# Reordering the first two batches of a fused attention and feed-forward kernel, with w_out read in 4 KB runs

## The chip, the cores and the metric

The kernel runs on one core of a Trainium2 chip. The metric is device microseconds (us) of one execution. Inputs are float32 and arrive in device memory; the output is float32. A ratio in this text is the mean time of one kernel's fast runs over the mean of the other kernel's fast runs of the same rounds, so it is not quite the ratio of the medians quoted beside it.

Engine names: PE is the matrix engine, PEld its weight loads, ACT the scalar engine, DVE the vector engine, POOL the general engine, SP the engine that issues nearly all DMA. PSUM is the memory that PE writes its results to; the other engines copy them out. Profile times count from the start of the profiled span.

## The reference, cut to what matters

```python
# q, k, v: (8 batches, 8 heads, 576 positions, 64)
q_s = softmax(q, over the 64)           # per row
k_s = softmax(k, over the 576)          # per column
kv  = k_s.T @ v                         # 64 x 64 per head
x   = q_s @ kv, heads side by side      # 4608 x 512
h   = x @ w_in                          # w_in 512 x 2048
g   = h * sigmoid(beta * h)
out = g @ w_out                         # w_out 2048 x 512
```

Nearly all the work is the two large products `h` and `out` (called `acc` below). For each of nine groups of 512 rows there are 64 matmuls of 128x512 for `h` and 64 for `acc`.

## The kernel before

Nine groups follow one another: one per batch for its first 512 positions, and one for the tails of all batches. While PE works on one group, ACT, DVE and POOL prepare the next one. The first group has no such cover. It needs its q, k and v, and the weights, which arrive in 512-wide blocks of w_in and w_out while it runs. Each block lands in float32 in one of four staging buffers and is then cast to bf16 into a tile that stays.

```python
w_in_b  = const.tile([P, KT, FF], BF16, name="w_in_b")     # 128 x 4 x 2048, one tile
w_out_d = moe_w_out.rearrange("(j p) f -> p j f", p=P)     # 2 KB runs
...
def w_cast(kind, blk, half, eng):
    if kind == "in":
        dst = w_in_b[:, :, ds(blk * 512 + half * 256, 256)]   # 256 columns of each kt
...
def mm_a(c, j, kts=None, tag=None):                        # h block j
    for kt in kts:
        nc.tensor.matmul(h[:], w_in_b[:, kt, ds(j * P, P)], x_of(c)[:, kt, :], ...)
    # then tanh on ACT, then (tanh + 1) * h on DVE -> g
def mm_b(c, j):                                            # acc += g block j @ w_out block j
...
tail_zero(0)
pool_cast(("out", 1), ("in", 2), ("out", 2))               # all casts of later blocks stand here,
tail_zero(1)                                               # ahead of h blocks 4 to 15
pool_cast(("in", 3), ("out", 3))
for u in range(4, NJ):
    mm_a(0, u) ...  mm_b(0, u - LAG) ...                   # and q, k, v of batch 1 in between
```

For the first two batches k and v of two heads lie on the two halves of the partitions. exp(k) is written into a zeroed 128x128 block diagonal, and nine 128-wide matmuls per head pair give kv.

The softmax here doesn't subtract the row's maximum and nothing guards it: scores larger than these inputs give would overflow.

## Time and profile before

| | before |
|---|---|
| median of 3 runs | 288.93 us (288.79 to 290.37) |
| profiled span | 286.8 us |
| PE busy | 97% |
| granted PE clock | 1.000 |
| first `h` matmul / first `acc` matmul | 15.24 / 20.11 us |
| first `h` matmul of batch 1 | 48.75 us |

First the page of the kernel before: the busy time per engine, then the span in 40 slices. A digit is a busy share in tenths; PEclk is the granted clock, DMA the busy share of the DMA engines.

```profile
span 286.8 us, 4132 instructions
...
PE 277.9 (97%) x1595; PEld 127.7 (45%) x1595; DVE 180.0 (63%) x280; ACT 162.9 (57%) x236; POOL 43.7 (15%) x58
...
PE   7799999999999999999999999999999999999994
...
PEclk9999999999999999999999999999999999999999
DMA  7999999809933963296319911893270033005004
```

PE has no hole after the first two slices. DMA is full over the first seven slices, which is the loading of q, k, v and the weights. Next are the groups of the `h` matmuls and of their weight loads (instructions, busy us, mean ns of one; then the idle time of the engine just ahead of them and what ended it).

```profile
L358 PE MATMUL h<-xT,w_in_b 128*128 128x512 bf16 x576 | 146.1, 379 | 0.5 <-ACT xT L143 0.2
...
L358 PEld LDWEIGHTS <-w_in_b 128*128 128x128 bf16 x576 | 55.3, 98 | 67.7 <-issue 2.7
```

The third view is the PE timeline (start, length, what, count).

```profile
20.11 1.89 PE L386 MATMUL acc<-w_out_b,g 128*128 128x512 bf16 x8
21.83 1.89 PE L358 MATMUL h<-xT,w_in_b 128*128 128x512 bf16 x8
23.56 1.89 PE L386 MATMUL acc<-w_out_b,g 128*128 128x512 bf16 x8
25.29 1.03 PE L358 MATMUL h<-xT,w_in_b 128*128 128x512 bf16 x4
...
39.02 0.61 PE L250 MATMUL tp<-identity,eq 128*128 128x128 bf16 x8 [0.62 <-ACT ek L158]
```

Four matmuls take 0.86 us from start to start. The last line has the one wait of note before batch 1, of 0.62 us.

### The profile page before, as it was taken

Reading aid. Unit: us, or ns where it says so; the run is one execution under the profiler, and the core shown is the slowest. Engines: PE = TensorE matmul, PEld = TensorE weight load, DVE = VectorE, ACT = ScalarE, POOL = GpSimd, SP = SyncE. Lnnn points to the kernel's source line nnn. Section 1 sums busy time; section 2 is a strip of 40 time slices with the busy share of each in tenths; the row PEclk is TensorE's granted clock in tenths of the full one; section 3 lists DMA queues with packets and bytes.
Section 4 is the critical chain, followed back from the end, with each engine's and each line's share of the span. In section 5 each row is a group of like instructions: output and inputs, shape, how many; then the busy total and the mean of one; then the engine's idle time right before and its main releaser. Section 6 shows DMA issues by size and latency. Waiting matters only on the chain.

```text
span 286.8 us, 4132 instructions
## 1 busy us (share of the span) xinstructions
PE 277.9 (97%) x1595; PEld 127.7 (45%) x1595; DVE 180.0 (63%) x280; ACT 162.9 (57%) x236; POOL 43.7 (15%) x58
## 2 busy tenths in 40 slices
PE   7799999999999999999999999999999999999994
PEld 2444445444444444444444444444445444444441
DVE  7954597695477457855694469456954695464432
ACT  4763586683496448734773568356835563553341
POOL 4458833300030020001200030003000000000000
PEclk9999999999999999999999999999999999999999
DMA  7999999809933963296319911893270033005004
GB/s 242 377 385 387 371 388 321 280 2 264 280 151 76 313 164 146 46 331 175 127 33 270 269 74 76 194 268 119 115 220 2 1 149 73 0 0 149 0 0 146
DMA packets 56227, 50.08 MB, mean 175 GB/s; under 512 B 26240, under 2 KB 47760, under 8 KB 56208
## 3 DMA queue, kind: packets, MB, share of 16 engines
q1 hardware_dynamic: 56064, 49.56, 55.8%
q8 instruction: 12, 0.20, 0.3%
q10 hardware_dynamic: 144, 0.26, 0.3%
q14 instruction: 7, 0.06, 0.1%
HBM read 36.71 MB, written 9.44 MB: 161 GB/s over the span
## 4 chain that ended last, share of the span: by engine, by line
PE 84%; DMA 11%; SPq 1%; POOL 1%; ACT 1%; issue 0%; DVE 0%; ACTq 0%
PE acc L386 40%; PE h L358 39%; DMA w_in<-in_moe_w_in_dram 6%; DMA k_st<-in_k_dram 5%; PE x L314 2%; PE kv L276 2%; POOL w_in_b L145 1%; PE kv L264 0%; PE tp L250 0%; SPq L85 0%; SPq L106 0%; PE x L318 0%; ACT ek L158 0%; DVE g L370 0%; ACT th L368 0%
## 5 line engine op out<-in xcount | busy, mean ns | idle before, releaser
L368 ACT ACTIVATE th<-h,beta_t 128x512 bf16<-128x512 f32 x144 | 98.5, 687 | 102.6 <-PE h L358 100.7
L370 DVE SCALAR_TENSOR_TENSOR g<-th,h 128x512 bf16<-128x512 bf16 x144 | 97.9, 682 | 92.2 <-ACT th L368 90.7
L358 PE MATMUL h<-xT,w_in_b 128*128 128x512 bf16 x576 | 146.1, 379 | 0.5 <-ACT xT L143 0.2
L386 PE MATMUL acc<-w_out_b,g 128*128 128x512 bf16 x576 | 145.9, 379 | 0.2 <-DVE g L370 0.2
L386 PEld LDWEIGHTS <-g 128*128 128x128 bf16 x576 | 56.0, 98 | 67.9 <-DVE g L370 1.0
L358 PEld LDWEIGHTS <-w_in_b 128*128 128x128 bf16 x576 | 55.3, 98 | 67.7 <-issue 2.7
L145 POOL CAST va<-v_st 128x2048 bf16<-128x2048 f32 (+2 forms) x12 | 17.3, 1460 | 145.0 <-DMA v_st<-in_v_dram 145.0
L225 DVE TENSOR_REDUCE rq<-eq 128x16 f32<-128x1024 bf16 x18 | 21.6, 1198 | 2.3 <-ACT eq L214 2.3
L231 DVE TENSOR_TENSOR eq<-eq,rq 128x1024 bf16<-128x1024 bf16 x18 | 22.6, 1257 | 0.1
L214 ACT ACTIVATE eq<-q_st 128x1024 bf16<-128x1024 f32 x16 | 16.3, 1048 | 2.9 <-DMA q_st<-in_q_dram 2.9
L143 ACT CAST xT<-x 128x512 bf16<-128x512 f32 x20 | 11.6, 585 | 11.1 <-PE x L314 10.3
L169 ACT ACTIVATE ek<-k_st 128x1024 bf16<-128x1024 f32 x12 | 12.6, 1047 | 0.0
L145 DVE COPY o<-acc 128x512 f32<-128x512 f32 x18 | 11.6, 683 | 0.9 <-PE acc L386 0.9
L314 PE MATMUL x<-qsT,kvp 128*128 128x512 bf16 x32 | 11.7, 380 | 0.4 <-DVE kvp L309 0.2
L145 DVE CAST xT<-x 128x512 bf16<-128x512 f32 x16 | 10.9, 684 | 0.5 <-PE x L314 0.5
L143 ACT COPY o<-acc 128x512 f32<-128x512 f32 x18 | 9.7, 591 | 2.6 <-PE acc L386 2.6
L158 ACT ACTIVATE ek<-k_st 64x576 bf16<-64x576 f32 x16 | 10.9, 679 | 0.4
L450 PE MATMUL warm<-kvp 128*128 128x512 bf16 x34 | 9.9, 432 | 1.2 <-DVE kvp L478 1.2
L145 POOL CAST w_out_b<-w_out 128x1024 bf16<-128x1024 f32 x8 | 8.2, 1040 | 6.6 <-DMA w_out<-in_moe_w_out_dram 6.5
L309 DVE TENSOR_TENSOR kvp<-kv,rk 64x256 bf16<-64x256 f32 (+2 forms) x24 | 8.0, 333 | 0.6
L145 POOL CAST w_in_b<-w_in 128x1024 bf16<-128x1024 f32 x7 | 7.2, 1040 | 3.5 <-DMA w_in<-in_moe_w_in_dram 3.4
L450 PEld LDWEIGHTS <-kvp 128*128 128x128 bf16 x34 | 3.4, 108 | 5.3 <-issue 2.1
(38 smaller groups left out, 67.1 us busy)
## 6 DMA issues: line engine op xcount, KB each, us to landing
out_dram<-o SPq DMA_DIRECT2D x14, 512.0 KB, 3.4
q_st<-in_q_dram SPq DMA_DIRECT2D x6, 1024.0 KB, 6.5
k_st<-in_k_dram SPq DMA_DIRECT2D x6, 1024.0 KB, 9.1
v_st<-in_v_dram SPq DMA_DIRECT2D x6, 1024.0 KB, 10.5
w_in<-in_moe_w_in_dram SPq DMA_DIRECT2D x3, 1024.0 KB, 9.7
k_st<-in_k_dram SPq DMA_DIRECT2D x8, 288.0 KB, 7.6
q_st<-in_q_dram SPq DMA_DIRECT2D x4, 512.0 KB, 7.8
w_out<-in_moe_w_out_dram SPq DMA_DIRECT2D x4, 512.0 KB, 9.5
```

What stands on the lines that cost most here:

```text
L143: eng.copy(dst, src)
L145: eng.tensor_copy(dst, src)
L169: nc.scalar.activation(ek[b][:, :, h, :].rearrange("p i h d -> p h i d"), k_st[b][:, h, 0 : R * D].rearrange("p h (i d) -> p h i d", i=R), ...
L214: nc.scalar.activation(eq[b][:, :, s * m : (s + 1) * m, :].rearrange("p i h d -> p h i d"), q_st[b][:, s * m : (s + 1) * m, :].rearrange(" ...
L225: nc.vector.tensor_reduce(rq[b][:, 0, :, h], eq[b][:, :, h, :], axis=AX.X, op=ALU.add)
L231: nc.vector.tensor_tensor(eq[b][:, :, h, :], eq[b][:, :, h, :], rq[b][:, 1, :, h].unsqueeze(3).to_broadcast((P, R, m, D)), ALU.mult,)
L314: nc.tensor.matmul(t[:], kvp[:, c, j, :], qsT[c][:, :, j, :])
L358: nc.tensor.matmul(h[:], w_in_b[:, kt, ds(j * P, P)], x_of(c)[:, kt, :], start=(kt == 0), stop=(kt == KT - 1),)
L368: nc.scalar.activation(th[:], h[:], ACTF.Tanh, scale=beta_t[:, j : j + 1])
L370: nc.vector.scalar_tensor_tensor(out=g[:], in0=th[:], scalar=1.0, in1=h[:], op0=ALU.add, op1=ALU.mult)
L386: nc.tensor.matmul(acc[st][:], g[:, ds(st * P, P)], w_out_b[:, j, :], start=(j == 0), stop=(j == NJ - 1),)
L450: nc.tensor.matmul(t[:, 0:cols], kvp[:, B - 1, 0, :], kvp[:, B - 1, :, :].rearrange("p j r -> p (j r)")[:, 0:cols],)
```

## The change

The intent has five parts. (1) In batches 0 and 1, exp(k) is dense, and kv is computed in two 64x64 quadrants of the array, so no zeroing is needed. (2) Batch 0 starts pair by pair: k and v of one head pair are loaded together, and exp, kv, norm and x follow per pair. (3) w_out is loaded in 4 KB runs, two neighbouring rows to a partition. The columns of `h` have to match, so the weight read of w_in takes every second column. (4) q of batch 1 is loaded ahead of the last weights and its k, v behind them. (5) The end of batch 0 interleaves kv and x of batch 1 with the last `h` and `acc` blocks.

The diff, cut to its core:

```diff
-    w_out_d = moe_w_out.rearrange("(j p) f -> p j f", p=P)
+    w_out_d = moe_w_out.rearrange("(hh p e) f -> p hh e f", p=P, e=2)
+    w_in_u = w_in_b[:].rearrange("p kt (hh q e) -> p kt hh e q", q=P, e=2)
@@ kv_mm, batches 0 and 1
-                    nc.tensor.matmul(t[:, jl, 0:D1], ek[b][:, j, i, :], va[b][:, j, i, :], ...)
+                    for e in range(2):
+                        r = slice(e * D, (e + 1) * D)
+                        nc.tensor.matmul(t[r, jl, 0:D1], ek[b][r, j, ds(i * D, D)], va[b][r, j, i, :],
+                                         ..., tile_position=(e * D, e * D))
@@ mm_a
-                w_in_b[:, kt, ds(j * P, P)],
+                w_in_u[:, kt, j // 2, j % 2, :],
@@ loads
-    load_q(0, parts=2); load_kv(k_st, k, 0, parts=4); load_kv(v_st, v, 0, parts=4); beta
+    q half 0; beta; then per pair j: k pair j, v pair j (q half 1 after pair 0)
-    in 0a, in 0b, out 0a, in 1, out 0b, out 1, in 2, out 2, in 3, q 1, out 3a, k 1, out 3b, v 1
+    in 0a, in 0b, out 0a, out 0b, in 1, out 1, in 2, out 2, q 1, in 3, out 3, k 1 and v 1 by pair
@@ batch 0, second part
-    mm_a 2, 3; mm_b 0, 1; casts of all later blocks; mm_a 4, 5; mm_b 2, 3; ...
+    mm_a 2, 3; casts of all later blocks; mm_b 0, 1, 2, 3; mm_a 4, 5; ...
+    (q transposes, kv, norm and x of batch 1 pair by pair among the last blocks)
```

(The lines under "loads" and "second part" are summaries; the rest is code shortened.)

More of the change, by code (lines that the diff above doesn't have):

```diff
@@ L58 @@
     beta_t = const.tile([P, NJ], F32, name="beta_t")
-    beta_r = const.tile([NJ, P], F32, name="beta_r")
-    ident16 = const.tile([NJ, NJ], F32, name="ident16")
+    beta_r = const.tile([NJ // 2, 2 * P], F32, name="beta_r")
+    ident8 = const.tile([NJ // 2, NJ // 2], F32, name="ident8")
     w_in_b = const.tile([P, KT, FF], BF16, name="w_in_b")
@@ L78, with load_q @@
     g_of, acc_of, att_of = {}, {}, {}
-    def load_q(b, parts=1):
-        t = stage.tile([P, H, R * D], F32, tag="q_st", bufs=2, name=f"q_st{b}")
+    def load_q(b, parts=1, only=None):
+        if b not in q_st:
+            q_st[b] = stage.tile([P, H, R * D], F32, tag="q_st", bufs=2, name=f"q_st{b}")
+        t = q_st[b]
         src = q[b, :, 0:MAIN, :].rearrange("h (p i) d -> p h (i d)", i=R)
         n = H // parts
-        for s in range(parts):
+        for s in range(parts) if only is None else (only,):
             nc.sync.dma_start(t[:, s * n : (s + 1) * n, :], src[:, s * n : (s + 1) * n, :])
-        q_st[b] = t
     def load_qtail():
@@ L97, in load_qtail, with load_kv @@
         q_st[B] = t
-    def load_kv(d, src, b, tag, parts=1):
-        t = stage.tile([P, H * (R + 1) * D], F32, tag=tag, bufs=2, name=f"{tag}{b}")
+    kv_st = {}
+    def load_kv(d, src, b, tag, pairs=None):
+        if (tag, b) not in kv_st:
+            kv_st[tag, b] = stage.tile([P, H * (R + 1) * D], F32, tag=tag, bufs=2, name=f"{tag}{b}")
+        t = kv_st[tag, b]
         if b < NW:
@@ L103, in load_kv @@
             sv = src[b].rearrange("(j e) (p i) d -> (e p) j (i d)", e=2, i=RW)
-            n = HP // parts
-            for s in range(parts):
-                nc.sync.dma_start(d[b][:, s * n : (s + 1) * n, :], sv[:, s * n : (s + 1) * n, :])
+            for j in range(HP) if pairs is None else pairs:
+                nc.sync.dma_start(d[b][:, j, :], sv[:, j, :])
         else:
@@ L126, in w_load @@
         else:
-            src = w_out_d[:, ds(4 * blk, 4), :]
-            c = slice(0, 4) if half is None else slice(half * 2, half * 2 + 2)
-            nc.sync.dma_start(t[:, c, :], src[:, c, :])
+            src = w_out_d[:, ds(2 * blk, 2)]
+            c = slice(0, 2) if half is None else slice(half, half + 1)
+            nc.sync.dma_start(t[:].rearrange("p (hh e) f -> p hh e f", e=2)[:, c], src[:, c])
     def w_cast(kind, blk, half, eng):
@@ L145, in evac, with ek_buf, kz_exp @@
             eng.tensor_copy(dst, src)
-    def ek_buf(b, eng=None):
-        t = work.tile([P, HP * RW * P], BF16, tag="ek", bufs=2, name=f"ek{b}")
+    def ek_buf(b):
+        t = work.tile([P, HP * RW * D], BF16, tag="ek", bufs=2, name=f"ek{b}")
         if b < NW:
-            ek[b] = t[:].rearrange("p (j i m) -> p j i m", j=HP, i=RW)
-            eng.memset(t[:].bitcast(F32), 0.0)
+            ek[b] = t[:].rearrange("p (j r) -> p j r", j=HP)
         else:
             ek[b] = t[:, 0 : R * H * D].rearrange("p (i h d) -> p i h d", i=R, h=H)
-    def kz_exp(b, j, m=1):
-        for e in range(2):
-            r = slice(e * D, (e + 1) * D)
-            nc.scalar.activation(
-                ek[b][r, j : j + m, :, e * D : (e + 1) * D],
-                k_st[b][r, j : j + m, :].rearrange("p j (i d) -> p j i d", i=RW),
-                ACTF.Exp,
-            )
+    def kz_exp(b, j):
+        if j == 0:
+            ek_buf(b)
+        nc.scalar.activation(ek[b][:, j, :], k_st[b][:, j, :], ACTF.Exp)
     def k_exp(b, s, n=2):
@@ L263, in kv_mm @@
                 for i in range(RW):
-                    nc.tensor.matmul(
-                        t[:, jl, 0:D1],
-                        ek[b][:, j, i, :],
-                        va[b][:, j, i, :],
-                        start=(i == 0),
-                        stop=(i == RW - 1),
-                    )
+                    for e in range(2):
+                        r = slice(e * D, (e + 1) * D)
+                        nc.tensor.matmul(
+                            t[r, jl, 0:D1],
+                            ek[b][r, j, ds(i * D, D)],
+                            va[b][r, j, i, :],
+                            start=(i == 0),
+                            stop=(i == RW - 1),
+                            tile_position=(e * D, e * D),
+                        )
                 continue
@@ L454, in warm @@
             )
-    load_q(0, parts=2)
-    load_kv(k_st, k, 0, "k_st", parts=4)
-    load_kv(v_st, v, 0, "v_st", parts=4)
-    nc.sync.dma_start(beta_r[:], moe_beta.rearrange("(j p) -> j p", p=P))
+    load_q(0, 2, 0)
+    nc.sync.dma_start(beta_r[:], moe_beta.rearrange("(hh q) -> hh q", q=2 * P))
+    for j in range(HP):
+        load_kv(k_st, k, 0, "k_st", [j])
+        load_kv(v_st, v, 0, "v_st", [j])
+        if j == 0:
+            load_q(0, 2, 1)
     w_load("in", 0, 0)
@@ L462 @@
     w_load("out", 0, 0)
+    w_load("out", 0, 1)
     w_load("in", 1)
-    w_load("out", 0, 1)
     w_load("out", 1)
@@ L467 @@
     w_load("out", 2)
+    load_q(1, 2)
     w_load("in", 3)
-    load_q(1, parts=2)
-    w_load("out", 3, 0)
-    load_kv(k_st, k, 1, "k_st", parts=4)
-    w_load("out", 3, 1)
-    load_kv(v_st, v, 1, "v_st", parts=2)
+    w_load("out", 3)
+    for j in range(HP):
+        load_kv(k_st, k, 1, "k_st", [j])
+        load_kv(v_st, v, 1, "v_st", [j])
     load_q(2)
@@ L479 @@
     make_identity(nc, identity[:])
-    make_identity(nc, ident16[:])
-    ek_buf(0, nc.vector)
+    make_identity(nc, ident8[:])
     nc.vector.memset(kvp[:, 0 : B - 1], 0.0)
     v_buf(0)
-    ek_buf(1, nc.gpsimd)
     v_buf(1)
@@ L500, in finish_b @@
                 store(c, st)
+    tb = ps.tile([P, 512], F32, tag="h", bufs=2, name="tb")
     warm(18)
-    for s in range(2):
-        q_exp(0, s)
-        q_sum(0, s)
-        q_mul(0, s)
-    for s in range(2):
-        for j in (2 * s, 2 * s + 1):
-            q_pet(0, j, nc.vector)
-        warm(10 if s == 0 else 2)
-    for j in range(HP):
-        kz_exp(0, j)
-    tb = ps.tile([P, 512], F32, tag="h", bufs=2, name="tb")
-    def attn0(p):
-        if 0 < p < 3:
-            warm(1, tag="acc3")
-        if p % 2 == 0:
-            vz_cast(0, p, nc.gpsimd)
-            vz_cast(0, p + 1, nc.gpsimd)
-        kv_mm(0, p, n=1, tag=f"acc{p}")
-        kv_norm(0, p, n=1)
@@ L525 @@
-    for p in range(HP):
-        attn0(p)
-        if p == 2:
-            w_cast("in", 0, 0, nc.gpsimd)
-        if p >= 1:
-            x_mm(0, p - 1, nc.scalar)
-        if p == 1:
-            nc.tensor.transpose(tb[:, 0:NJ], beta_r[:], ident16[:])
-            nc.scalar.copy(beta_t[:], tb[:, 0:NJ])
-        if p >= 2:
-            for j in range(2):
-                mm_a(0, j, [p - 2])
-    x_mm(0, HP - 1, nc.scalar)
-    for kind, blk in (("in", 0), ("out", 0)):
-        for half in range(2):
-            if (kind, half) not in (("in", 0), ("out", 1)):
-                w_cast(kind, blk, half, nc.gpsimd)
@@ L542 @@
-    for kt in (2, 3):
-        for j in range(2):
-            mm_a(0, j, [kt])
-    w_cast("in", 1, 0, nc.vector)
-    w_cast("in", 1, 1, nc.gpsimd)
+    q_exp(0, 0)
+    q_sum(0, 0)
+    q_mul(0, 0)
+    kz_exp(0, 0)
+    vz_cast(0, 0, nc.gpsimd)
+    nc.tensor.transpose(tb[:, 0 : NJ // 2], beta_r[:, 0 : 2 * P : 2], ident8[:])
+    nc.tensor.transpose(tb[:, NJ // 2 : NJ], beta_r[:, 1 : 2 * P : 2], ident8[:])
+    nc.scalar.copy(
+        beta_t[:].rearrange("p (hh e) -> p e hh", e=2),
+        tb[:, 0:NJ].rearrange("p (e hh) -> p e hh", e=2),
+    )
@@ new lines @@
+    kv_mm(0, 0, n=1, tag="acc0")
+    kv_norm(0, 0, n=1)
+    q_exp(0, 1)
+    warm(5)
+    q_pet(0, 0, nc.scalar)
+    q_pet(0, 1, nc.scalar)
+    q_sum(0, 1)
+    q_mul(0, 1)
+    kz_exp(0, 1)
+    vz_cast(0, 1, nc.gpsimd)
+    warm(3)
+    kv_mm(0, 1, n=1, tag="acc1")
+    x_mm(0, 0, nc.scalar)
+    kv_norm(0, 1, n=1)
+    kz_exp(0, 2)
+    vz_cast(0, 2, nc.gpsimd)
+    warm(3)
+    kv_mm(0, 2, n=1, tag="acc2")
+    kv_norm(0, 2, n=1)
+    x_mm(0, 1, nc.scalar)
+    kz_exp(0, 3)
+    vz_cast(0, 3, nc.gpsimd)
@@ new lines, with w_cast_kt @@
+    q_pet(0, 2, nc.scalar)
+    q_pet(0, 3, nc.vector)
+    warm(2)
+    kv_mm(0, 3, n=1, tag="acc3")
+    kv_norm(0, 3, n=1)
+    x_mm(0, 2, nc.scalar)
+    x_mm(0, 3, nc.scalar)
+    def w_cast_kt(kind, blk, half, eng):
+        t = wst[kind, blk]
+        c = ds(half * 256, 256)
+        for kh in range(2):
+            evac(eng, w_in_b[:, 2 * kh : 2 * kh + 2, ds(blk * 512 + half * 256, 256)], t[:, 2 * kh : 2 * kh + 2, c])
+    w_cast_kt("in", 0, 0, nc.gpsimd)
+    w_cast("in", 0, 1, nc.gpsimd)
@@ L547 @@
+    w_cast("out", 0, 0, nc.gpsimd)
     w_cast("out", 0, 1, nc.gpsimd)
-    mm_a(0, 2)
-    mm_a(0, 3)
-    mm_b(0, 0)
-    mm_b(0, 1)
     def pool_cast(*what):
@@ L562, in tail_zero @@
             nc.gpsimd.memset(vt[t][ds(e * TAIL, TAIL), e, :, D:D1], 2.0)
+    for kt in range(KT):
+        for j in range(2):
+            mm_a(0, j, [kt])
+    mm_a(0, 2)
+    mm_a(0, 3)
+    w_cast("in", 1, 0, nc.vector)
+    w_cast("in", 1, 1, nc.gpsimd)
     tail_zero(0)
@@ L567 @@
     pool_cast(("in", 3), ("out", 3))
-    for u in range(4, NJ):
-        if u != 5:
-            mm_a(0, u)
-        if u == 4:
-            mm_a(0, 5)
-            mm_b(0, 2)
-            continue
-        if u == 13:
-            for j in (0, 1):
-                q_pet(1, j, nc.vector)
-        mm_b(0, u - LAG)
-        if u in (10, 11):
-            q_exp(1, u - 10)
-        if u in (10, 12):
-            q_sum(1, (u - 10) // 2)
-        if u in (11, 13):
-            q_mul(1, (u - 11) // 2)
-        if u >= 12:
-            kz_exp(1, u - 12)
-    vz_cast(1, 0, nc.gpsimd, m=2)
-    vz_cast(1, 2, nc.gpsimd, m=2)
-    for j in (2, 3):
-        q_pet(1, j, nc.vector)
-    mm_b(0, NJ - 2)
-    kv_mm(1, 0)
-    kv_norm(1, 0)
-    warm(2)
-    kv_mm(1, 1)
-    kv_norm(1, 1)
+    for j in range(HP):
+        vz_cast(1, j, nc.gpsimd)
+    for j in range(4):
+        mm_b(0, j)
+    mm_a(0, 4)
+    mm_a(0, 5)
+    for u in range(6, NJ):
+        mm_a(0, u)
+        if u in (9, 10):
+            q_exp(1, u - 9)
+        if u in (9, 11):
+            q_sum(1, (u - 9) // 2)
+        if u in (10, 12):
+            q_mul(1, (u - 10) // 2)
+        if u in (12, 14):
+            for j in (u - 12, u - 11):
+                q_pet(1, j, nc.vector)
+        if u >= 13:
+            kz_exp(1, u - 13)
+        if u >= 14:
+            kv_mm(1, u - 14, n=1)
+            kv_norm(1, u - 14, n=1)
+        mm_b(0, u - 2)
+    kz_exp(1, 3)
+    kv_mm(1, 2, n=1)
+    kv_norm(1, 2, n=1)
+    x_mm(1, 0, nc.scalar)
+    mm_b(0, NJ - 2)
+    x_mm(1, 1, nc.vector)
+    kv_mm(1, 3, n=1)
+    kv_norm(1, 3, n=1)
+    x_mm(1, 2, nc.scalar)
     mm_b(0, NJ - 1)
-    for j in range(HP):
-        x_mm(1, j, nc.scalar if j % 2 == 0 else nc.vector, tag="h" if j < 2 else "att")
+    for kt in range(2):
+        for j in range(2):
+            mm_a(1, j, [kt])
+    x_mm(1, 3, nc.scalar)
     for st in range(R):
         store(0, st)
-    for kt in range(KT):
+    for kt in (2, 3):
         for j in range(2):
```

## The prediction

> **What bounds the kernel now.** The page gives PE 97% busy, and the chain of waits is 79% the two feed-forward matmul lines. From 48.75 us (first `h` matmul of batch 1) to the end the timeline shows PE back to back, 0.86 us per four 128x512 matmuls. The change leaves that part alone, so it can win only before 48.75 us. There the chain names DMA instead: 11% of the span (k 6.0 us, w_in 6.8 and 10.2, k 8.9). DMA is at 99% in nearly every slice of 2.5–50 us, about 385 GB/s. Landing times, from the casts that waited: w_in's first half 14.1, w_out block 2 29.7, first half of w_out block 3 36.8, k of batch 1 37.5, its v 42.6.
>
> **What changes.**
> 1. Bytes before 50 us are the same. w_out comes in 4 KB instead of 2 KB runs; the trace moves 2 KB weight runs at 385 GB/s already, so I expect nothing from this. To pay for it the w_in columns become a stride-2 weight load. Weight loads take 98 ns and hide under 216 ns per matmul; the Trainium skill ("TensorE: Matmul & The Clock Gate", Weight-path perf modes) says the fast read takes packed or strided chunks. Expected cost 0; not shown by any trace here.
> 2. Dense exp(k): 8 calls of 0.68 us become 4 per batch, and two memsets (2.0 us DVE, 2.1 us POOL) go. 2.7 us of ACT per batch saved, but half of it was hidden behind loads.
> 3. kv: 9 matmuls at 31 ns per pair become 18 quarter-array ones. The later batches' half-width ones run at about 17 ns each, so a tie, unless the two row halves cannot write one PSUM bank at once (the skill's "TensorEngine Tiling", PSUM Pressure); then +0.3 us per pair.
> 4. The first batch becomes a chain per pair: exp(k), kv, norm, x, evacuation, with ACT also taking three of four q transposes (0.55 us each). Worked out with the trace's durations: exp of k pair 1 ends at 10.9, pair 2 at 12.9, pair 3 at 14.9, the last x about 17.1. So PE starts `h` at about 16.3 (before: 15.24), but then runs dense; the first `acc` matmul comes at about 19.8 (before: 20.11).
> 5. q of batch 1 before the last weights: w_in block 3 now lands at about 35.3 us (11.8 MB at the measured rate), castable at 36.4. PE would want it at 35.3 (before, it began u=12 at 35.65): a new stall of about 1 us.
> 6. End of batch 0: the 0.62 us transpose wait, 0.43 us of warm-up matmuls and the block of four x matmuls go; kv, x and acc are interleaved. New waits there: exp(k) pair 2 queues behind the last tanh (0.4 us), x 2 waits for x 1's PSUM buffer (0.5 us).
>
> **Sum.** Entry to batch 1: −1.5 us of removed waits and work, +0.75 for the later weights, +0.5 for new waits: about −0.3 us.
>
> **Prediction: 288.5 us, 286.8 to 290.2 (8 in 10).** Faster by over 2%: 0.01; within 2%: 0.96; slower: 0.03.
>
> **What would show it.** First `acc` matmul near 19.8; an idle PE of 0.5–1.2 us at about 35 us released by the w_in cast after DMA; batch 1's `h` matmuls under way with all four x tiles at 48–49 us; weight loads still near 98 ns; `h` matmuls 216 ns apart; 18 kv matmuls within 0.5 us.
>
> **What would make it wrong.** Strided weight loads that slow the matmuls (576 of them: much slower). Quadrant matmuls serialising (+1 to 2 us). 4 KB runs that really speed the loads, which would remove the stall at 35 us (down to about 286). The early gaps on PE lowering the granted clock.

## More of the kernel before

The kernel text gives the order of work on each engine. The framework then adds the waits between engines, from which tile ranges each instruction reads and writes. POOL takes its casts in the order of the text, so they may stand far ahead of their use at no cost, as long as each reader waits for its own cast alone.

## The result, and the profile after

The changed kernel took 308.91 us (median of 4, 306.84 to 310.63) against 288.94 us for the kernel before. The ratio is 1.0679, with a 95% interval of 1.0628 to 1.0729. It is correct, and 19.6 us slower (0.0679 of 288.9). The prediction, 288.5 us with a range of 286.8 to 290.2, was wrong.

The page of the changed kernel (its profiled run is the slowest of the four, 310.63 us):

```profile
span 308.8 us, 4271 instructions
...
PE 283.9 (92%) x1665; PEld 129.5 (42%) x1665; DVE 178.8 (58%) x281; ACT 159.3 (52%) x232; POOL 44.4 (14%) x60
...
PE   7683199699999999999999999999999999999994
...
PEclk9998579879999999999999999999999999999999
DMA  7999999003079439535933791289517032104003
```

PE has a hole in the fourth and fifth slices (23 to 39 us). The granted clock falls there, and once more around 54 to 70 us. From then on the profile is that of before. The groups of the `h` matmuls and of their weight loads:

```profile
L361 PE MATMUL h<-xT,w_in_b 128*128 128x512 bf16 x576 | 148.8, 385 | 12.3 <-POOL w_in_b L150 12.1
...
L361 PEld LDWEIGHTS <-w_in_b 128*128 128x128 bf16 x576 | 56.1, 99 | 81.6 <-POOL w_in_b L150 12.4
```

The idle time ahead of `h` matmuls grew from 0.5 to 12.3 us, and 12.1 us of that is one wait for a POOL cast into w_in_b. A weight load itself still takes 98 to 99 ns. The PE timeline around it:

```profile
18.30 3.62 PE L361 MATMUL h<-xT,w_in_b 128*128 128x512 bf16 x16
21.76 3.62 PE L389 MATMUL acc<-w_out_b,g 128*128 128x512 bf16 x16
25.21 0.38 PE L361 MATMUL h<-xT,w_in_b 128*128 128x512 bf16 x1
37.66 4.72 PE L361 MATMUL h<-xT,w_in_b 128*128 128x512 bf16 x11 [12.07 <-POOL w_in_b L150]
42.22 1.03 PE L389 MATMUL acc<-w_out_b,g 128*128 128x512 bf16 x4
```

One matmul of `h` block 4 runs, and the second waits until 37.66 us. The eleven matmuls after the wait take 4.56 us up to the next start (42.22 us), where 2.4 would do at 0.216 us each. The POOL timeline (bracket: idle time before, and its releaser) says which cast ended the wait:

```profile
22.05 1.04 POOL L150 CAST w_in_b<-w_in 128x1024 bf16<-128x1024 f32 x1 [1.72 <-PE h L361]
...
27.24 2.02 POOL L150 CAST w_in_b<-w_in 128x1024 bf16<-128x1024 f32 x2
...
35.59 2.02 POOL L150 CAST w_in_b<-w_in 128x1024 bf16<-128x1024 f32 x2 [2.12 <-DMA w_in<-in_moe_w_in_dram]
```

The cast that block 4 does need is that of the first half of w_in block 1. It runs on DVE, and block 4's first weight load waits for it (first line from the DVE timeline, second from that of PEld):

```profile
23.29 1.78 DVE L150 CAST w_in_b<-w_in 128x1024 bf16<-128x1024 f32 x1
```

```profile
25.12 0.10 PEld L361 LDWEIGHTS <-w_in_b 128*128 128x128 bf16 x1 [0.24 <-DVE w_in_b L150]
```

That was over at 25.1 us (the second half, which blocks 6 and 7 read, at 23.1 us on POOL). The wait ends at 37.6 us, with the last cast of block **3**. No arithmetic asks for that.

The built programs say the same without any run. These are the weight loads of `h` block 4, second contraction slice, with the cast that each waits for (offsets and steps in elements; the tile holds 4 slices of 2048 columns):

```
before:   reads offset 2560, 128 x step 1   no wait for a POOL cast
changed:  reads offset 2560, 128 x step 2   waits for the POOL cast that writes
                                            offset 1792, 4 slices x step 2048, 256 columns
```

That cast writes columns 1792 to 2047 of each slice. The read takes columns 512 to 766 of slice 1. They share no element. But the range from the cast's first element (1792) to its last (8191) contains the read (2560 to 2814). In the kernel before the same cast is no obstacle to the contiguous read, though that read (2560 to 2687) lies inside the same outer range. So the outer range counts here only where the read is strided too; why the framework compares in this way is not shown. In the changed kernel later `h` blocks have no wait for a w_in cast of their own, because this one covered them all. The first slice of block 4 (offset 512) lies ahead of the outer range, and indeed it is the one matmul that ran at 25.21 us.

### The profile page after: what moved, and what is told of

The parts are those of the page before. It is cut to its first block, busy times and chain, and to the rows that moved or that the text cites. A ratio compares the mean times of both kernels' runs of the same rounds, so it can differ in the third digit from the quotient of the medians.

```text
span 308.8 us, 4271 instructions
## 1 busy us (share of the span) xinstructions
PE 283.9 (92%) x1665; PEld 129.5 (42%) x1665; DVE 178.8 (58%) x281; ACT 159.3 (52%) x232; POOL 44.4 (14%) x60
## 4 chain that ended last, share of the span: by engine, by line
PE 81%; DMA 9%; DVE 4%; POOL 2%; SPq 1%; ACT 1%; issue 1%; POOLq 0%
PE h L361 39%; PE acc L389 38%; DMA w_in<-in_moe_w_in_dram 7%; DMA k_st<-in_k_dram 2%; PE x L317 2%; PE kv L279 1%; DVE eq L231 1%; DVE g L373 1%; POOL w_in_b L150 1%; DVE rq L225 1%; PE kv L266 1%; SPq L111 1%; ACT eq L214 0%; DVE qsT L150 0%; PE x L321 0%
## 5 line engine op out<-in xcount | busy, mean ns | idle before, releaser
L361 PE MATMUL h<-xT,w_in_b 128*128 128x512 bf16 x576 | 148.8, 385 | 12.3 <-POOL w_in_b L150 12.1
L361 PEld LDWEIGHTS <-w_in_b 128*128 128x128 bf16 x576 | 56.1, 99 | 81.6 <-POOL w_in_b L150 12.4
L150 POOL CAST va<-v_st 128x576 bf16<-128x576 f32 (+1 forms) x14 | 18.4, 1313 | 160.5 <-DMA v_st<-in_v_dram 160.5
L231 DVE TENSOR_TENSOR eq<-eq,rq 128x1024 bf16<-128x1024 bf16 x18 | 23.4, 1298 | 0.1
L148 ACT CAST xT<-x 128x512 bf16<-128x512 f32 x21 | 12.3, 586 | 12.2 <-PE x L317 11.4
L214 ACT ACTIVATE eq<-q_st 128x1024 bf16<-128x1024 f32 x16 | 16.3, 1047 | 4.2 <-DMA q_st<-in_q_dram 4.2
L312 DVE TENSOR_TENSOR kvp<-kv,rk 64x64 bf16<-64x64 f32 (+1 forms) x28 | 8.6, 308 | 0.7
L266 PE MATMUL kv<-va,ek 64*64 64x65 bf16 x144 | 4.3, 206 | 4.4 <-POOL va L150 1.7
L150 POOL CAST w_in_b<-w_in 128x1024 bf16<-128x1024 f32 (+1 forms) x8 | 7.3, 933 | 5.0 <-DMA w_in<-in_moe_w_in_dram 3.3
L266 PEld LDWEIGHTS <-ek 64*64 64x64 bf16 x144 | 3.4, 118 | 7.8 <-issue 3.7
```

The costliest lines, as they stand in the source:

```text
L148: eng.copy(dst, src)
L150: eng.tensor_copy(dst, src)
L214: nc.scalar.activation(eq[b][:, :, s * m : (s + 1) * m, :].rearrange("p i h d -> p h i d"), q_st[b][:, s * m : (s + 1) * m, :].rearrange(" ...
L231: nc.vector.tensor_tensor(eq[b][:, :, h, :], eq[b][:, :, h, :], rq[b][:, 1, :, h].unsqueeze(3).to_broadcast((P, R, m, D)), ALU.mult,)
L266: nc.tensor.matmul(t[r, jl, 0:D1], ek[b][r, j, ds(i * D, D)], va[b][r, j, i, :], start=(i == 0), stop=(i == RW - 1), tile_position=(e * D, ...
L361: nc.tensor.matmul(h[:], w_in_u[:, kt, j // 2, j % 2, :], x_of(c)[:, kt, :], start=(kt == 0), stop=(kt == KT - 1),)
```

## The experiments

**Theory A**: the waits for a strided read are set by the outer bounds of the ranges, so block 4 waits for every cast that the text puts ahead of it. **Rival B**: w_in block 3 truly comes too late, since q of batch 1 goes ahead of it. (The prediction's own step 5 named it, at 1 us.) **Rival C**: the quarter-array matmuls or the early gaps lower the granted clock, and the stall is a by-product.

All twelve runs were correct. Medians, and ratios to the kernel before of the same rounds:

| run | us | ratio | 95% interval |
|---|---|---|---|
| changed kernel | 308.91 | 1.0679 | 1.0628–1.0729 |
| split_tiles | 294.18 | 1.0168 | 1.0150–1.0186 |
| no_stride | 294.12 | 1.0168 | 1.0144–1.0191 |
| block_major | 293.95 | 1.0168 | 1.0154–1.0181 |
| before_4k_only | 303.35 | 1.0495 | 1.0468–1.0522 |
| w_in3_first | 305.38 | 1.0559 | 1.0535–1.0582 |
| layout_only | 289.41 | 1.0009 | 0.9997–1.0022 |
| newstart_oldrest | 290.40 | 1.0043 | 1.0029–1.0057 |
| oldstart_newrest | 293.03 | 1.0132 | 1.0114–1.0150 |
| end_as_before | 290.60 | 1.0041 | 1.0024–1.0059 |
| acc23_later | 292.84 | 1.0129 | 1.0115–1.0142 |
| before_4k_split | 288.79 | 0.9989 | 0.9976–1.0003 |
| best | 287.94 | 0.9966 | 0.9947–0.9985 |

The kernel before had medians of 289.11 to 289.15 us in these rounds.

### The stall: split_tiles, no_stride, before_4k_only, w_in3_first, block_major

**split_tiles** cuts one tile into eight and changes nothing else of the changed kernel:

```diff
-    w_in_b = const.tile([P, KT, FF], BF16, name="w_in_b")
+    w_in_b = [const.tile([P, KT, 256], BF16, name=f"w_in_h{i}") for i in range(8)]
-                w_in_u[:, kt, j // 2, j % 2, :],
+                w_in_u[j // 2][:, kt, j % 2, :],      # still every second column
```

> The changed kernel with nothing altered but w_in_b cut into eight tiles of 256 columns (same strided weight reads, same loads, same casts, same order). Theory A (the strided weight read of block 4 is ordered after every cast that was written ahead of it, because two strided ranges are compared by their outer bounds; 12.1 us false wait): the wait before h block 4 falls below 0.5 us, the acc matmuls start at 21.8 as before, the mean clock is back above 0.99, total 289 to 292 us. Rival B (w_in block 3 really comes too late because q of batch 1 goes ahead): the wait stays at 10 us or more wherever it stands, total above 300. Rival C (quarter-array matmuls or early gaps lower the granted clock, the stall is a by-product): clock stays near 0.97, total 297 or more.

Measured: 294.18 us. The PE timeline of split_tiles:

```profile
21.75 3.62 PE L389 MATMUL acc<-w_out_b,g 128*128 128x512 bf16 x16
25.20 1.89 PE L361 MATMUL h<-xT,w_in_h 128*128 128x512 bf16 x8
27.72 1.02 PE L361 MATMUL h<-xT,w_in_h 128*128 128x512 bf16 x4 [0.64 <-DVE g L373]
28.58 1.03 PE L389 MATMUL acc<-w_out_b,g 128*128 128x512 bf16 x4
```

From 8.92 to 25.20 us it is the run of the changed kernel to within 0.02 us, and then the wait is not there. Mean clock 0.991 in place of 0.966. B and C fall as causes of the stall. The total is 2 us above what A expected, so something else is left.

**no_stride** undoes the 4 KB part alone (contiguous weight reads, w_out in 2 KB runs, one tile):

```diff
-    w_out_d = moe_w_out.rearrange("(hh p e) f -> p hh e f", p=P, e=2)
+    w_out_d = moe_w_out.rearrange("(j p) f -> p j f", p=P)
-                w_in_u[:, kt, j // 2, j % 2, :],
+                w_in_b[:, kt, ds(j * P, P)],
```

> The changed kernel with the 4 KB part alone undone (w_out in 2 KB runs, contiguous weight reads, one w_in_b tile, beta as before). Theory A: no wait before h block 4, total within 1 us of split_tiles (289 to 292). If the 4 KB runs speed the loads, split_tiles is the faster by up to 1 us. Rival B: wait of 10 us stays, since the order of loads is unchanged; total above 300. Rival C: clock stays near 0.97.

Measured: 294.12 us, the same ratio as split_tiles, and like it 2 us above the expectation. So, as far as the intervals can tell, the whole effect of part (3) in the changed kernel is the false wait. The wait that is left at block 4 is short, and is for the cast of its own columns (PE timeline of no_stride):

```profile
26.16 1.90 PE L360 MATMUL h<-xT,w_in_b 128*128 128x512 bf16 x8 [0.80 <-DVE w_in_b L149]
```

That cast took 2.83 us on DVE in this profile and 1.78 us in that of split_tiles; no run was made to explain this.

**before_4k_only** puts the lines of part (3) into the kernel before:

```diff
-                w_in_b[:, kt, ds(j * P, P)],
+                w_in_u[:, kt, j // 2, j % 2, :],
     (and w_out_d, its load, beta as in the change)
```

> The kernel before with the 4 KB part alone (w_out in 4 KB runs, stride-2 weight reads, one w_in_b tile). Theory A: a wait of about 13 us before h block 4 (from about 22 us to the end of the last w_in cast, near 35.4), then some matmuls at half clock; total 303 to 307. Rival B and C: about 289, since loads stand in the old order and no quarter-array matmul is there.

Measured: 303.35 us. The PE timeline of before_4k_only:

```profile
21.83 3.09 PE L359 MATMUL h<-xT,w_in_b 128*128 128x512 bf16 x7 [2.36 <-DVE w_in_b L146]
24.75 1.89 PE L387 MATMUL acc<-w_out_b,g 128*128 128x512 bf16 x8
26.48 0.38 PE L359 MATMUL h<-xT,w_in_b 128*128 128x512 bf16 x1
35.52 3.08 PE L359 MATMUL h<-xT,w_in_b 128*128 128x512 bf16 x7 [8.66 <-POOL w_in_b L146]
```

The stall is there with old loads and no quarter-array matmul, in two pieces. The second ends with the last w_in cast at 35.5 us. The first is the same false order against an earlier cast: `h` block 2 waits for the DVE cast of block 1, which the text of the kernel before puts ahead of it. Together they are 11.0 us, less than the 13 us expected, because 5 us of work lay between them.

**w_in3_first** restores one place in the order of loads:

```diff
-    load_q(1, 2)
     w_load("in", 3)
+    load_q(1, 2)
```

> The changed kernel with w_in block 3 loaded ahead of q of batch 1 again. Theory A: the wait stays but ends with the earlier last cast, near 35.5 instead of 37.7 us, so it is about 10 us, total 306 to 307. Rival B: the wait vanishes, total about 290.

Measured: 305.38 us, 0.6 us under the expectation. The PE timeline of w_in3_first:

```profile
35.80 4.88 PE L361 MATMUL h<-xT,w_in_b 128*128 128x512 bf16 x11 [10.09 <-POOL w_in_b L150]
```

The wait is 10.09 us and ends at 35.80 us, 1.9 us sooner. The stall follows the landing of the last block, and block 4 does not need that block. That is A, and the order of loads only sets how long it is.

**block_major** keeps one tile and strided reads, but stores the tile block by block, so that each cast writes one contiguous range:

```diff
-    w_in_b = const.tile([P, KT, FF], BF16, name="w_in_b")
+    w_in_b = const.tile([P, FF // 256, KT, 256], BF16, name="w_in_b")
```

> The changed kernel with w_in_b still one tile and the weight reads still strided, but stored block by block (block, kt, column instead of kt, column), so that each cast writes one contiguous range and no read's outer bounds cross another block. Theory A (outer bounds): the 12 us wait is gone, as with eight tiles, total 293.5 to 295. If the cure of split_tiles was the number of tiles and not the bounds: still 305 or more.

Measured: 293.95 us. First blocks 4 and 5 in the PE timeline of block_major, then the one wait for a weight cast in its list of PE's waits (us in total, times, longest):

```profile
24.29 1.89 PE L361 MATMUL h<-xT,w_in_b 128*128 128x512 bf16 x8
```

```profile
PE h L361 <- POOL w_in_b L150: 1.5, 1, 1.5
```

The wait at block 4 is gone. The 1.5 us, at 38.85 us, are `h` block 12 waiting for the cast of its own columns, in w_in block 3: a true wait, taken up again at step 5 of the prediction below. In the built program each block's reads now wait for their own cast. So the bounds decide it, and not the number of tiles. A is shown from both sides.

### The clock after the stall

The weight loads of the changed kernel just behind the wait (PEld timeline):

```profile
37.66 0.13 PEld L361 LDWEIGHTS <-w_in_b 128*128 128x128 bf16 x2 [12.44 <-POOL w_in_b L150]
38.06 0.15 PEld L361 LDWEIGHTS <-w_in_b 128*128 128x128 bf16 x1 [0.28 <-issue]
38.49 0.15 PEld L361 LDWEIGHTS <-w_in_b 128*128 128x128 bf16 x1 [0.28 <-issue]
38.92 0.15 PEld L361 LDWEIGHTS <-w_in_b 128*128 128x128 bf16 x1 [0.28 <-issue]
```

They come 0.43 us apart in place of 0.216, and the stretches view gives a granted clock of 0.51 from 37.66 to 42.22 us. The Trainium skill ("TensorE: Matmul & The Clock Gate", Part 1) says that an idle window of about 3.4 us drops the array to half rate and that about 3.4 us of sustained work restores it. The half rate agrees with this trace, which has it after 12.07 us of idle. The times agree only roughly: full rate came back after 4.56 us here, and after 2.92 us in before_4k_only, where waits of 0.67 and 2.36 us with five matmuls between them had been enough for the half rate (clock 0.50 from 21.83 to 24.75 us). The slow clock costs 2.2 us more. A second slow stretch (clock 0.81 from 57.99 to 75.98 us) follows shorter waits at the end of batch 0. It does not need the stall, since the profile of split_tiles has one at the same place in the program (clock 0.60 from 45.33 to 49.60 us). Its cause is open: no_stride has a wait of 1.34 us there, and its clock stays at 1.00.

### The 5 us that are left: layout_only, newstart_oldrest, oldstart_newrest, end_as_before, acc23_later

Without the stall the change still loses 0.0168, which is 4.9 us. **Theory D**: it sits in the program order, partly in the new start and partly in the rest of batch 0. **Rival E**: the quadrants cost. **Rival F**: it is all the start, or the start is absorbed later. The next four runs have contiguous weight reads, like no_stride.

**layout_only** puts the layout part alone into the kernel before:

```diff
-            eng.memset(t[:].bitcast(F32), 0.0)                # block diagonal, 9 full matmuls
+        nc.scalar.activation(ek[b][:, j, :], k_st[b][:, j, :], ACTF.Exp)   # dense, 18 quadrant matmuls
```

> The kernel before with the layout part alone: dense exp(k) (4 calls for 8, no memsets) and kv in 64x64 quadrants; loads, order and w_out as before. Theory D (the 5 us that split_tiles still loses sit in the program order: about 1.6 in the new start, the rest between the first acc and batch 1; the layout itself costs nothing): 288.2 to 289.0 us, the 0.6 us transpose wait at 39 us gone. Rival E (quadrant kv matmuls cost through slower matmuls or a lower clock): 290 or more.

Measured: 289.41 us, a tie (the interval holds 1). My figure was a little too good, since the transposes' wait did not go: it is 0.92 us in this profile. E falls, and the layout gains nothing either. The kv matmuls of one pair in both kernels (the first line is from the PE timeline of before, the second from that of the changed kernel):

```profile
12.46 0.45 PE L264 MATMUL kv<-va,ek 128*128 128x65 bf16 x9
```

```profile
12.56 0.48 PE L266 MATMUL kv<-va,ek 64*64 64x65 bf16 x18 [0.87 <-ACT ek L162]
```

Twice as many matmuls take about the same time. (The next matmul does start later: 0.41 us after the first of them, at 12.97 us, against 0.29 us before.) The skill's "TensorEngine Tiling" warns (Restrictions and Gotchas, PSUM Pressure) that different row tiles cannot access one PSUM bank at the same time. Here the two row halves write one bank, each its own partitions, and the two matmuls of a pair start 3 to 4 ns apart; the results are correct, and no serialising shows at 0.48 us for 18.

**newstart_oldrest** has the layout and the new start, and everything after the first two `h` blocks as before:

```diff
-    w_load("out", 0, 1); w_load("in", 1); ...; load_q(1, 2); w_load("in", 3); ...
+    w_load("in", 1); w_load("out", 0, 1); ...; w_load("in", 3); load_q(1, parts=2); ...
     (new order of batch 0's start kept; from mm_a(0, 2) on, the text of before)
```

> no_stride with all from the second h blocks on (loads of weights and batch 1, order of h, acc, q, kv, x) put back as before; new only the layout and the pairwise start. Theory D: first acc at about 21.7 us (before 20.1), total 290 to 291. Rival F (the start's delay is absorbed later because the loads bound batch 0 anyway): about 289.

Measured: 290.40 us. Over layout_only the new start costs 0.0034, or 1.0 us. It delays the first `acc` to 21.19 us in this profile (21.76 in that of the changed kernel).

**oldstart_newrest** is the reverse, no_stride with the start of before:

```diff
-    q half 0, beta, (k, v) by pair; pairwise exp, kv, norm, x      # new start
+    q, k, v in three blocks; the order of work of before           # old start
```

> no_stride with the start put back as before (loads of batch 0 in three blocks, its order of work); new the layout and all from the second h blocks on. Theory D: first acc near 20.1 us, waits of 0.6 us or more before the third h pair and at the first kv of batch 1 remain, total 291 to 293. Rival F: the whole loss was the start, total about 289.

Measured: 293.03 us, so the rest costs 0.0123, or 3.6 us, over layout_only. With 1.0 for the start and 0.3 for the layout the sum is 4.9 us, which is no_stride. D holds, though with 1.0 us for the start and not the 1.6 that it expected, and F falls.

**end_as_before** is oldstart_newrest with the end of batch 0 put back:

```diff
-        if u >= 14:
-            kv_mm(1, u - 14, n=1); kv_norm(1, u - 14, n=1)    # one pair at a time among h and acc
+    kv_mm(1, 0); kv_norm(1, 0); warm(2); kv_mm(1, 1); kv_norm(1, 1)    # after the loop, two pairs at a time
```

> oldstart_newrest with the end of batch 0 (q exp to transpose, kv, x of batch 1 among the last h and acc) put back as before; loads and the early acc order stay new. Theory D: of the 3.9 us of the rest, about 2.4 lie in this end, so 290.4 to 291.0, and no wait of kv for the q transpose copies. If the later weights (q of batch 1 first) are the cost: 292.5 or more, with a wait for w_in casts.

Measured: 290.60 us, so the interleaved end costs 0.0091, or 2.6 us. The PE timeline of oldstart_newrest shows its waits:

```profile
42.05 0.71 PE L249 MATMUL tp<-identity,eq 128*128 128x128 bf16 x8
43.99 0.48 PE L265 MATMUL kv<-va,ek 64*64 64x65 bf16 x18 [1.24 <-DVE qsT L149]
...
48.38 0.39 PE L316 MATMUL x<-qsT,kvp 128*128 128x512 bf16 x1 [0.25 <-DVE kvp L311]
...
50.63 0.38 PE L316 MATMUL x<-qsT,kvp 128*128 128x512 bf16 x1 [0.38 <-DVE xT L149]
```

The transposes, kv and x all take turns in two PSUM buffers. Right behind the transposes kv waits for DVE to copy them out, while DVE is busy with `g` and with scaling q. In the old end an `acc` block stands in between and hides that. The three waits sum to 1.9 of the 2.6 us. This cause is read from the trace: no run gave these stages more buffers. What is left of the rest is 0.0032 (0.9 us) between end_as_before and layout_only, which no run isolates.

**acc23_later** moves one pair of blocks in oldstart_newrest:

```diff
-    for j in range(4):
-        mm_b(0, j)
-    mm_a(0, 4); mm_a(0, 5)
+    mm_b(0, 0); mm_b(0, 1); mm_a(0, 4); mm_a(0, 5); mm_b(0, 2); mm_b(0, 3)
```

> oldstart_newrest with acc blocks 2 and 3 put after h blocks 4 and 5, as before the change. Theory D: the 0.63 us wait of h block 6 for its PSUM buffer goes, total 292.2 to 292.6. If h 4 then waits for the w_in block 1 cast instead (it lands later now), the gain is nil: 293.

Measured: 292.84 us, no gain (0.0003). The 0.63 us wait for a PSUM buffer is gone. In its place `h` block 4 waits 0.67 us for the cast of w_in block 1. In the new text that cast stands on DVE behind `g` of blocks 2 and 3, which DVE finishes at 21.85 us, and then it waits 0.20 us for its load, which now comes behind the second half of w_out block 0. The early acc blocks cover that later cast, and without them one wait takes the other's place.

### Is anything in the change worth having? before_4k_split, best

**before_4k_split** is the kernel before with part (3) and eight tiles for w_in_b, so without a false wait:

```diff
-    w_in_b = const.tile([P, KT, FF], BF16, name="w_in_b")
+    w_in_b = [const.tile([P, KT, 256], BF16, name=f"w_in_h{i}") for i in range(8)]
     (and the lines of part (3))
```

> The kernel before with the 4 KB w_out runs and stride-2 weight reads, and w_in_b in eight tiles, so that no false wait can arise. If 4 KB runs and strided reads are worth nothing: 288.5 to 289.4, weight loads 98 ns. If 4 KB runs speed the loads: down to 287.5, w_out and w_in casts earlier than in before by 0.3 us or more. If strided weight reads cost: above 290 and matmuls over 216 ns apart.

Measured: 288.79 us, ratio 0.9989 with 1 inside the interval. Strided weight reads and 4 KB runs are worth nothing that these runs can tell. In its trace the weight casts on POOL start within 0.22 us of those of the kernel before, some earlier and some later, so the 4 KB runs do not visibly speed the loads. The skill ("TensorE: Matmul & The Clock Gate", Weight-path perf modes) says the fast weight read takes its chunks packed or strided. That agrees: in split_tiles, where nothing stalls, the 576 strided loads have a mean of 98 ns, as the contiguous ones of before.

**best** takes two small things out of before_4k_split that the traces had shown on the critical path:

```diff
-        if u == 13:
-            for j in (0, 1): q_pet(1, j, nc.vector)
         mm_b(0, u - LAG)
+        if u == 13:
+            for j in (0, 1): q_pet(1, j, nc.vector)
...
     kv_mm(1, 0); kv_norm(1, 0)
-    warm(2)
     kv_mm(1, 1); kv_norm(1, 1)
```

> before_4k_split with the first two q transposes of batch 1 moved behind the acc block of the same step and the two warm-up matmuls between the kv pairs of batch 1 taken out. If these are real idle and filler on the critical path: 0.6 and 0.4 us less, total 287.6 to 288.2. If kv pair 2 then waits for its v cast, or the transposes' copies are late: 288.8 as before_4k_split.

Measured: 287.94 us, ratio 0.9966 (0.9947 to 0.9985), the only version here that is clearly faster than the kernel before, by 0.3%. The PE timeline of best:

```profile
38.56 1.03 PE L387 MATMUL acc<-w_out_b,g 128*128 128x512 bf16 x4
39.42 0.61 PE L251 MATMUL tp<-identity,eq 128*128 128x128 bf16 x8
...
47.91 3.72 PE L359 MATMUL h<-xT,w_in_h 128*128 128x512 bf16 x16
```

The 0.62 us wait ahead of the transposes is gone, and batch 1 starts at 47.91 us in place of 48.75. Both changes were run together, so their shares are not separated.

## Why the prediction was wrong, point by point

The loss of 19.6 us splits as follows, from ratios times 289.1 us. Changed kernel minus split_tiles: 14.8 us, the false wait with the slow clock behind it. Layout: 0.3. Start: 1.0. Rest of batch 0: 3.6.

- **Step 1, "Expected cost 0; not shown by any trace here"**: this is the step that failed. It costed the strided weight read as an instruction, and there it was right (98 ns, hidden). It did not ask what the strided range does to the waits. The term put at 0 measured 14.8 us: 12.07 us of idle PE and 2.2 us of half clock in the profile (that of the slowest of the four executions); the remaining 0.5 us is not attributed. The list of what would make the prediction wrong had "much slower" only for slow loads. The wait stood in the built program, and it was the one thing that the source lines did not show. The skill's "Perfetto Trace Analysis" (Identifying Dependency Chains) says to look at an instruction's text for the semaphores it waits on. The queries before the prediction are all of the kernel before, so none shows the waits of the changed one.
- **Steps 2 and 3, layout and quadrants, "a tie"**: right. The measured ratio is 1.0009.
- **The 4 KB runs, "I expect nothing from this"**: right. The measured ratio is 0.9989, not told from 1.
- **Step 4, the pairwise start**: right that it starts `h` later, and mis-sized. Predicted first `h` 16.3 and first `acc` 19.8 us; measured 18.30 and 21.76. The chain was already late at its head. The second half of q was exponentiated from 9.18 us, and the first kv ran at 8.94 us because its v had landed only at 7.39 us and the cast took 1.49 us. The second and fourth pairs' casts took 0.67 us. Its own figures implied a gain of 0.3 us (first `acc` at 19.8 for 20.11); it costs 1.0.
- **Step 5, a stall of about 1 us for w_in block 3**: right in some profiles only. With the false wait out of the way PE reaches that block at 38.08 us in split_tiles, and its first half had been cast by 36.7, so there is no stall. In oldstart_newrest, where PE comes sooner, it is about 0.2 us, in acc23_later 0.31 us, and in block_major 1.5 us. Even so the ratios of split_tiles and block_major are the same (1.0168).
- **Step 6, the end of batch 0**: the sign was wrong. I counted about 1 us of work and waits taken out and 0.9 us of new waits. It measured 2.6 us of loss. I had not counted the 1.24 us in which the first kv waits for the transposes' PSUM buffer.

The sum "about −0.3 us" would thus have been wrong by some 5 us without the false wait too, outside the stated range.

## What to carry to other kernels

A change of access pattern is also a change of dependences: after making a read strided, list in the built program what each reader waits for, and give regions that are filled separately their own tile or a layout in which each fill is one contiguous range. Where casts stand in the text far ahead of their use, a single false range overlap can turn them all into one barrier, as it did here. Before small stages are interleaved finely among large matmuls, count the buffers that they share: with two PSUM buffers shared by transposes, kv and x, hand-overs became waits (1.24, 0.25 and 0.38 us here).

## What the Trainium skill lacked or had wrong

- No page has it: waits that a framework sets for strided ranges by their outer bounds. Here it was one wait of 12.07 us (changed kernel), and no such wait with block-wise storage of the same data. It is a fact of the software and not of the chip.
- "TensorEngine Tiling" (Restrictions and Gotchas): the rule that row tiles cannot access one PSUM bank at the same time did not show. 18 quadrant matmuls of both row halves into one bank (each half its own partitions) took 0.48 us, 9 full ones took 0.45 us, and the results were correct.
- "TensorE: Matmul & The Clock Gate" (Part 1): its idle window of about 3.4 us is no lower limit. Waits of 0.67 and 2.36 us with five matmuls between them were followed by half rate in before_4k_only, and full rate came back after 2.92 us there and 4.56 us in the changed kernel.
- "TensorE: Matmul & The Clock Gate" (Weight-path perf modes) gives a range of allowed strides but no time for a strided weight load. Here 576 of them at stride 2 had a mean of 98 ns, the same as contiguous ones.
